# Attention and two dense layers on one core: a third early operand buffer, output copies on one engine, and new durations in the plan

## The chip, the cores and the metric

The kernel runs on one core of one Trainium2 chip. The metric is the device time of one execution in microseconds (us); lower is better. A core has a matmul engine (TensorE, PE in the rows, with its weight loads as PEld), VectorE (DVE), ScalarE (ACT), GpSimd (POOL) and SyncE (SP), which here issues the transfers between memory and on-chip buffers.

## What is computed

Attention over blocks of 64 tokens (a token sees its own block and all earlier ones), then a gated layer, then a second layer with the activation called ELU, all in 32-bit floats:

```python
scores = scale * q @ k.T            # 4 batches, 8 heads, 576 tokens, 64 channels
attn = softmax(where(block_i >= block_j, scores, -1e9)) @ v
x = attn as (2304 tokens, 512)
g = x @ w_gate; val = x @ w_val     # 512 -> 1536
y = (g * sigmoid(g) * val) @ w_out  # 1536 -> 512, the first output product
h = y @ w_in                        # 512 -> 2048
out = where(h > 0, h, exp(min(h, 0)) - 1) @ w_out2   # 2048 -> 512
```

## The kernel before

**Split products.** Every operand of a large product is cut into a high half, rounded to the matmul engine's own 32-bit form, and a low half, the rest. A product is three matmuls: high x high, high x low, low x high (`mm3`, L163 to L166). Making the halves is the work of the other engines: ACT writes the high half, DVE or POOL subtracts it for the low one.

**Stages.** (1) Attention for chunks of 256 tokens, and beside it the gate and value products, called gv; their result is stored in the scratch tensor a_scr. (2) The first output product, called p2: five chunks (four of 512 tokens, one of 256), each of 12 units, one for each block of 128 of the 1536 channels. A unit loads its operand (`ar`, L663), ACT writes `ah` (L666), DVE writes `al` (L669), and the PE issues 4 x 3 matmuls into four accumulators y. The ring of ah and al has three slots, so unit n can be split once unit n - 3 has been multiplied. Two of the slots lie in space that comes free when attention ends (`to_w1`), the third in space that comes free when gv ends (`to_p2`). After 12 units `p2_drain` copies the four accumulators to `ys` (L708), two on ACT and two on DVE, and SP stores them to y_scr. (3) The second layer, called p3, for three groups of 768 tokens and 8 pairs of channel blocks each. It uses a seven-product scheme for 2 x 2 blocks: `p3_y` combines and splits y (L749, L757, L758), `p3_weights` does the same for the input weights (L793, L801, L804, stored in w_scr), `p3_h` multiplies, adds up on DVE (L854, seven sums to a pair), applies ELU (L845 to L848) and splits the result into `gh` (ACT, L849) and `gl` (DVE, L851). `p3_o` multiplies by the output weights of the pair before.

**Weights** arrive as 64-bit floats. `conv_unit` turns one block into 32-bit: a load of 512 KB (`raw`), one step on ACT (L142), three on DVE (L150, L152, L154), and for a plain weight the high half on ACT (L157) and the low one on POOL (L161). There are 68 such units: 24 for gate and value, 12 for the first output weights (`wo`, tiles woh and wol), 32 for the last two weights. A unit of the last output weight is converted into place during p2 if its pair is below NE, else during p3.

**What sets the order.** `Plan` is a list scheduler that runs when the program is built. Each task has an engine, a duration in ns written in the code, a priority and its dependences; `Plan.order` walks through time and always starts the ready task of the best priority. From this comes one fixed order of instructions on each engine. On the chip each engine takes its instructions in that order and waits at each for what it needs. The durations in the code decide only the order; the chip's own decide the time.

Of the kernel before, what the change touches and what calls it, by code (L numbers as in the profile page):

```python
# [8 lines left out]
F32 = mybir.dt.float32  # L9
# [25 lines left out]
GF, NACT, NFP, XLP = 4, 20, 8, False  # L35
NFILL, PFILL, WARM = 40, 1e9, 7000.0
CLEAD2, CLEAD3 = 5.0, 100.0
HT, NG, HP, PAIR3, NP, NW, NE = 384, 3, K2 // 2, 15.4, 9, 8, 5
LAT, SELF, DMA_IN, DMA_OUT = 300.0, 100.0, 1300.0, 900.0


# [69 lines left out]
def attention_moe_moe_kernel(ctx: ExitStack, tc: tile.TileContext,  # L111
# [116 lines left out]
    def conv_unit(i, prio, after=(), whole=False):  # L228
        r, c, w = ("raw", i, 0), ("c", i, 0), ("w", i, 0)
        add("SP", 450, lambda: cv_dma(i), prio, writes=[r], data=1456)  # L230
        add("ACT", 520, lambda: cv_a(i), prio, [r], [c])
        for p, ns in enumerate((335, 602, 602)):
            add("DVE", ns, lambda p=p: cv_b(i, p), prio, [r, c], [c])
        if whole:
            return
        add("ACT", 520, lambda: cv_hi(i), prio, [c], [w], after)
        add("POOL", 1330, lambda: cv_lo(i), prio, [c, w], [w])


    qz = [t0.tile([128, H, 128], F32, name=f"qz{u}") for u in range(2)]  # L240
# [416 lines left out]
    def p2_prep(i, T, f):  # L657
        u, v = nxt("ar"), nxt("ah")
        late = [("p2", 0, 0)]

        def load():
            for j in range(T // CH):
                sp.dma_start(out=ar_b[u % 5][:, CH * j:CH * j + CH], in_=a_scr[2 * i + j][f])  # L663

        def hi():
            act.activation(ah_b[v % 3][:, 0:T], ar_b[u % 5][:, 0:T], ACTF.Copy, scale=0.5)  # L666

        def lo():
            dve.scalar_tensor_tensor(al_b[v % 3][:, 0:T], ar_b[u % 5][:, 0:T], 0.5, ah_b[v % 3][:, 0:T].bitcast(F32), ALU.mult, ALU.subtract)  # L669

        ark, ahk = ("ar", u, 0), ("ah", v, 0)
        add("SP", 450 * (T // CH), load, PMP, [("a", (2 * i + j) * K1 + f // 2 * 2, 0) for j in range(T // CH)], [ark],
            [("w1", 0, 0)] if u < 3 else late, data=T * 1.42)
        add("ACT", .833 * T + 93, hi, PMP, [ark], [ahk], [] if v < 2 else late)
        add("DVE", 1.04 * T + 68, lo, PMP, [ark, ahk], [("ah", v, 1)])
        return v

    yacc = {}
# [23 lines left out]
    def p2_drain(i, T):  # L702
        for m in range(KD):
            u = nxt("ys")
            yk, k = ("y", i * KD + m, 0), ("ys", u, 0)

            def cp(eng, m=m, u=u):
                eng(ys_b[u % 4][:, 0:T], yacc[i, m][:, 0:T])  # L708

            def spill(g, c, t, n, m=m, u=u):  # L710
                sp.dma_start(out=y_scr[g][m, :, c:c + n], in_=ys_b[u % 4][:, t:t + n])

            plan.group = "p2"
            add(*(("ACT", .833 * T + 90, lambda cp=cp: cp(act.copy)) if m % 2 else ("DVE", 1.04 * T + 68, lambda cp=cp: cp(dve.tensor_copy))), PMP,
                [yk], [k], [("p2", 0, 0)])
            for x in p2_parts(i, T):
                add("SP", 450, lambda x=x, spill=spill: spill(*x), PMP, [k], [("yscr", x[0], (m, i))], data=x[3] * 1.42)
            plan.group = None
# [64 lines left out]
    def p3_weights(p, prio):  # L783

        i = unit["i", 2 * p]
        for u in range(2):
            conv_unit(i + u, prio, whole=True)
        part = lambda r, c: cv_state[i + r][1][:, 256 * c:256 * c + 256]
        ck = lambda r, c: ("c", i + r, c)
        whole = [("c", i, 0), ("c", i + 1, 0)]  # L790

        def comb(d, x, y, op):
            add("DVE", 400, lambda: dve.tensor_tensor(part(*d), part(*x), part(*y), op), prio, [ck(*x), ck(*y)] + whole, [ck(*d)])  # L793

        def split(o, x):
            n = nxt("wm")
            hk, lk = ("wm", n, 0), ("wm", n, 1)

            def hi():
                wm[n] = hand["wp"].tile([128, 2, 256], F32R, tag="wm", name="wm", bufs=3)  # L800
                act.copy(wm[n][:, 0], part(*x))  # L801

            add("ACT", 400, hi, prio, [ck(*x)] + whole, [hk], [("p2", 0, 0)])
            add("POOL", 850, lambda: pool.tensor_tensor(wm[n][:, 1], part(*x), wm[n][:, 0].bitcast(F32), ALU.subtract), prio, [ck(*x), hk] + whole, [lk])  # L804
            add("SP", 450, lambda: sp.dma_start(out=w_scr[p][o], in_=wm[n].bitcast(F32).rearrange("p h f -> p (h f)")), prio - 1,
                [hk, lk], [("wscr", p, o)], data=728)
# [12 lines left out]
        split(6, a11)
# [11 lines left out]
    def p3_h(i, p, ns, due):  # L831
# [7 lines left out]
        def elu(src, sk, name):  # L839
# [4 lines left out]
            g = lambda k: gp[v % NP][k]  # L844
            add("ACT", 500, lambda: act.activation(t(), src(), ACTF.Tanh, scale=0.5), PMP, [sk], [tk], first)  # L845
            add("ACT", 500, lambda: act.activation(e(), src(), ACTF.Exp), PMP, [sk], [ek])
            add("DVE", 540, lambda: dve.scalar_tensor_tensor(t(), e(), 1.0, t(), ALU.add, ALU.mult), PMP, [tk, ek], [tk])  # L847
            add("DVE", 540, lambda: dve.scalar_tensor_tensor(t(), t(), 0.0, src(), ALU.min, ALU.max), PMP, [tk, sk], [tk])  # L848
            add("ACT", 480, lambda: act.copy(g(0), t()), PMP, [tk], [hk], first)  # L849
            eng, en = dve, "DVE"  # L850
            add(en, 1100 if eng is pool else 540, lambda: eng.tensor_tensor(g(1), t(), g(0).bitcast(F32), ALU.subtract), PMP, [tk, hk], [lk])  # L851

        def plus(b, x, d):
            add("DVE", 520, lambda: dve.tensor_tensor(hc(d), hb[b][:, 0:HT], hc(x), ALU.add), PMP, [hbk(b), hck(x)], [hck(d)])  # L854

        for o, j in enumerate(OSEQ):
            b = (7 * q + o) % 2 if q or o < 2 else o
# [73 lines left out]
    def to_w1():  # L931
        attn.release()
        at_ps.release()
        hand["st2"] = sb("st2", 1, "right")
        p2_bufs(hand["st2"], (0, 1, 2), (0, 1))
        hand["w1"] = sb("w1", 1, "right")
        hand["y_ps"] = ps("y_ps", 1, "right")
        for g in range(K1):
            WOH[g] = hand["w1"].tile([128, DM], F32R, name=f"woh{g}")
            WOL[g] = hand["w1"].tile([128, DM], F32R, name=f"wol{g}")  # L940
            cv_units[2 * K1 + g] = (wo[g], WOH[g], WOL[g])

    def to_p2():
        hand["wgvB"].release()
# [3 lines left out]
        gv_ps.release()  # L948
        hand["st3"] = sb("st3", 1)
        p = hand["st3"]  # L950
        p2_bufs(p, (3, 4), (2,))
        ys_b.extend(p.tile([128, 512], F32, name=f"ys{k}") for k in range(4))
        p = hand["wp"] = sb("wp", 1)
        for f in range(2 * NE):
# [154 lines left out]
```

## Time and profile before

| | us |
|---|---|
| median of 3 runs | 1061.53 (1060.5 to 1070.12) |
| the profiled execution | 1062.92 |
| its span, first to last instruction | 1061.2 |
| PE busy | 1030.2 |
| DVE busy | 837.1 |
| ACT busy | 599.2 |
| POOL busy | 292.7 |

Busy time is an average over stages with different limits: what a change in one stage is worth is read in that stage's stretch. Matmuls overlap and their ends are modelled, so the steps from start to start tell more than PE's busy time. The granted clock is full (1.00) in every stretch quoted below.

### The profile page before, as it was taken

How to read it: one execution, taken by the hardware profiler on the slowest of the kernel's cores; microseconds unless marked ns; L12 is line 12 of the kernel's file. 1: busy time of each engine (PE TensorE's matmuls, PEld its weight loads, DVE VectorE, ACT ScalarE, POOL GpSimd, SP SyncE). 2: the span in 40 equal slices, each digit the busy share in tenths (PEclk: the TensorE clock that was granted, in tenths of full speed). 3: DMA queues.
4: the chain of work that ended last, by engine and by line, in shares of the span. 5: the costliest groups of instructions: out<-in, count | busy, mean ns of one | idle time of the engine just before them, and what ended most of it. 6: DMA issues, size and time to landing. Idle time of an engine off the chain costs nothing. (4 is left out here: it accounts for less than half of the span.)

```text
span 1061.2 us, 19577 instructions
## 1 busy us (share of the span) xinstructions
PE 1030.2 (97%) x6520; PEld 934.1 (88%) x6520; DVE 837.1 (79%) x1977; ACT 599.2 (56%) x1521; POOL 292.7 (28%) x288
## 2 busy tenths in 40 slices
PE   8999899999999999999999999999999999999998
PEld 7678899999999999999877778888988989898997
DVE  6689998888888888878777787798678665876664
ACT  4688787777776776654454544545344433543342
POOL 1268544443443344303234333331000000000000
PEclk8899999999999999999999999999999999999999
DMA  7487556432442244014799888874446434454331
GB/s 176 135 232 208 159 165 185 119 90 86 125 126 85 87 125 119 32 54 147 248 328 313 299 274 304 300 234 129 120 133 215 128 111 119 129 169 114 115 109 61
DMA packets 119366, 170.00 MB, mean 160 GB/s; under 512 B 15840, under 2 KB 75744, under 8 KB 119264
## 3 DMA queue, kind: packets, MB, share of 16 engines
q1 hardware_dynamic: 119264, 168.74, 52.5%
q8 instruction: 52, 0.85, 0.3%
q14 instruction: 50, 0.41, 0.1%
HBM read 130.42 MB, written 38.27 MB: 159 GB/s over the span
## 5 line engine op out<-in xcount | busy, mean ns | idle before, releaser
L164 PE MATMUL gv<-xh,wh 128*128 128x256 f32 x864 | 257.1, 298 | 1.1 <-DVE as L645 0.8
L165 PE MATMUL gv<-xl,wh 128*128 128x256 f32 x864 | 242.4, 281 | 0.1
L166 PE MATMUL gv<-xh,wl 128*128 128x256 f32 x864 | 242.1, 280 | 0.0
L164 PEld LDWEIGHTS gv<-xh,wh 128*128 128x128 f32 x864 | 164.2, 190 | 7.4 <-issue 4.3
L165 PEld LDWEIGHTS gv<-xl,wh 128*128 128x128 f32 x864 | 164.3, 190 | 0.5 <-DVE xl L604 0.3
L166 PEld LDWEIGHTS gv<-xh,wl 128*128 128x128 f32 x864 | 164.0, 190 | 0.0
L854 DVE TENSOR_TENSOR ys<-h,ys 128x384 f32<-128x384 f32 x162 | 88.0, 554 | 83.4 <-PE h L166 78.4
L845 ACT ACTIVATE ar<-ys 128x384 f32<-128x384 f32 x96 | 50.5, 526 | 134.0 <-DVE ys L854 111.9
L164 PE MATMUL h<-yo,ws 128*128 128x384 f32 x326 | 110.0, 337 | 1.9 <-DVE ys L854 1.7
L165 PE MATMUL h<-yo,ws 128*128 128x384 f32 x326 | 110.0, 337 | 0.0
L166 PE MATMUL h<-yo,ws 128*128 128x384 f32 x326 | 109.6, 336 | 0.0
L165 PE MATMUL y<-al,woh 128*128 128x512 f32 (+1 forms) x240 | 89.5, 373 | 5.8 <-DVE al L669 5.7
L409 POOL TENSOR_TENSOR ks<-rk,ks 64x576 fp32r<-64x576 f32 (+1 forms) x56 | 70.7, 1262 | 88.1 <-ACT ks L406 46.9
L164 PE MATMUL y<-ah,woh 128*128 128x512 f32 (+1 forms) x240 | 88.9, 370 | 2.3 <-ACT ys L708 1.0
L166 PE MATMUL y<-ah,wol 128*128 128x512 f32 (+1 forms) x240 | 88.4, 368 | 0.0
L804 POOL TENSOR_TENSOR wm<-c,wm 128x256 fp32r<-128x256 f32 x56 | 55.5, 1002 | 96.9 <-ACT wm L801 87.1
L894 PE MATMUL o<-oh,gl 128*128 128x512 f32 x198 | 78.8, 398 | 1.8 <-DVE gl L851 1.6
L893 PE MATMUL o<-ol,gh 128*128 128x512 f32 x198 | 78.1, 395 | 0.0
L892 PE MATMUL o<-oh,gh 128*128 128x512 f32 x198 | 77.1, 389 | 0.5 <-ACT gh L849 0.5
L542 DVE TENSOR_TENSOR tl<-tr,th 128x256 fp32r<-128x256 f32 x176 | 69.1, 415 | 6.9 <-ACT th L538 6.1
L538 ACT CAST th<-tr 128x256 fp32r<-128x256 f32 x176 | 61.3, 376 | 22.5 <-PE tr L534 20.6
L422 POOL TENSOR_TENSOR vs<-rv,vs 128x320 fp32r<-128x320 f32 (+1 forms) x56 | 48.0, 857 | 94.1 <-ACT vs L418 80.9
(150 smaller groups left out, 2654.1 us busy)
## 6 DMA issues: line engine op xcount, KB each, us to landing
ws<-w_scr SPq DMA_DIRECT2D x168, 256.0 KB, 2.7
w_scr<-wm SPq DMA_DIRECT2D x56, 256.0 KB, 3.8
a_scr<-as SPq DMA_DIRECT2D x54, 256.0 KB, 2.4
ar<-a_scr SPq DMA_DIRECT2D x108, 128.0 KB, 3.7
rk<-in_kt_dram SPq DMA_DIRECT2D x32, 288.0 KB, 4.4
raw<-in_w2i_dram SPq DMA_DIRECT2D x16, 512.0 KB, 4.5
raw<-in_w2o_dram SPq DMA_DIRECT2D x16, 512.0 KB, 5.0
rq<-in_qt_dram SPq DMA_DIRECT2D x60, 128.0 KB, 3.9
```

Source lines behind the costliest of these rows:

```text
L164: pe.matmul(dst, wh, xh, start=start, stop=False)
L165: pe.matmul(dst, wh, xl, start=False, stop=False)
L166: pe.matmul(dst, wl, xh, start=False, stop=stop)
L409: pool.tensor_tensor(st["ks"][64:128, 0:ext], raws[i][0][64:128, j, 0:ext], st["ks"][64:128, 0:ext].bitcast(F32), ALU.subtract)
L538: act.copy(st["th", c], st["tr", c][:, 0:QW])
L542: dve.tensor_tensor(st["tl", c], st["tr", c][:, 0:QW], st["th", c].bitcast(F32), ALU.subtract)
L804: add("POOL", 850, lambda: pool.tensor_tensor(wm[n][:, 1], part(*x), wm[n][:, 0].bitcast(F32), ALU.subtract), prio, [ck(*x), hk] + whole, ...
L845: add("ACT", 500, lambda: act.activation(t(), src(), ACTF.Tanh, scale=0.5), PMP, [sk], [tk], first)
L854: add("DVE", 520, lambda: dve.tensor_tensor(hc(d), hb[b][:, 0:HT], hc(x), ALU.add), PMP, [hbk(b), hck(x)], [hck(d)])
L892: pe.matmul(d, h, OH[f], start=(p == 0 and u < 2), stop=False)
L893: pe.matmul(d, h, OL[f], start=False, stop=False)
L894: pe.matmul(d, l, OH[f], start=False, stop=(p == HP - 1 and u > 1))
```

## The change

Five things are changed. The third slot of ah and al is allocated with the other two when attention ends; in return the last of the twelve wo tiles is allocated, and its halves are written, only when gv has ended (`wo_alloc`). All copies of `p2_drain` go to ACT. The plan's durations are raised for what runs from the wo units on: the conversion's three DVE steps, the low halves on POOL, `al`, the weight recombination, and DVE's steps of p3. NE goes from 5 to 3, so four more units of the last output weight (two pairs) are converted in p3 and not in p2. NP, the number of gate slots in p3, goes from 9 to 8.

```diff
-HT, NG, HP, PAIR3, NP, NW, NE = 384, 3, K2 // 2, 15.4, 9, 8, 5
+HT, NG, HP, PAIR3, NP, NW, NE = 384, 3, K2 // 2, 15.4, 8, 8, 3
...
-        for p, ns in enumerate((335, 602, 602)):
+        for p, ns in enumerate((335, 602, 602) if i < 2 * K1 else (500, 700, 750)):
             add("DVE", ns, lambda p=p: cv_b(i, p), prio, [r, c], [c])
...
-        add("POOL", 1330, lambda: cv_lo(i), prio, [c, w], [w])
+        add("POOL", 1330 if i < 2 * K1 else 1500, lambda: cv_lo(i), prio, [c, w], [w])
...
-        add("ACT", .833 * T + 93, hi, PMP, [ark], [ahk], [] if v < 2 else late)
-        add("DVE", 1.04 * T + 68, lo, PMP, [ark, ahk], [("ah", v, 1)])
+        add("ACT", .833 * T + 93, hi, PMP, [ark], [ahk], [] if v < 3 else late)
+        add("DVE", 1.3 * T + 68, lo, PMP, [ark, ahk], [("ah", v, 1)])
...
-            add(*(("ACT", .833 * T + 90, lambda cp=cp: cp(act.copy)) if m % 2 else ("DVE", 1.04 * T + 68, lambda cp=cp: cp(dve.tensor_copy))), PMP,
-                [yk], [k], [("p2", 0, 0)])
+            add("ACT", .833 * T + 90, lambda cp=cp: cp(act.copy), PMP, [yk], [k], [("p2", 0, 0)])
...
-            add("DVE", 400, lambda: dve.tensor_tensor(part(*d), part(*x), part(*y), op), prio, [ck(*x), ck(*y)] + whole, [ck(*d)])
+            add("DVE", 500, lambda: dve.tensor_tensor(part(*d), part(*x), part(*y), op), prio, [ck(*x), ck(*y)] + whole, [ck(*d)])
```

In the same way the plan's 850 becomes 1000 for the weight split on POOL (L804), 540 becomes 575 for the three DVE steps of ELU and its split, and 520 becomes 560 for the sums (L854). The buffers:

```diff
     def to_w1():
...
-        p2_bufs(hand["st2"], (0, 1, 2), (0, 1))
+        p2_bufs(hand["st2"], (0, 1, 2), (0, 1, 2))
...
-        for g in range(K1):
-            WOH[g] = hand["w1"].tile([128, DM], F32R, name=f"woh{g}")
-            WOL[g] = hand["w1"].tile([128, DM], F32R, name=f"wol{g}")
-            cv_units[2 * K1 + g] = (wo[g], WOH[g], WOL[g])
+        for g in range(K1 - 1):
+            wo_alloc(hand["w1"], g)
+
+    def wo_alloc(p, g):
+        WOH[g] = p.tile([128, DM], F32R, name=f"woh{g}")
+        WOL[g] = p.tile([128, DM], F32R, name=f"wol{g}")
+        cv_units[2 * K1 + g] = (wo[g], WOH[g], WOL[g])
 
     def to_p2():
...
-        p2_bufs(p, (3, 4), (2,))
+        p2_bufs(p, (3, 4), ())
+        wo_alloc(p, K1 - 1)
...
-        conv_unit(2 * K1 + g, due2[0, g] - CLEAD2, after=[("w1", 0, 0)])
+        conv_unit(2 * K1 + g, due2[0, g] - CLEAD2, after=[("w1" if g < K1 - 1 else "p2", 0, 0)])
```

Since the durations steer the plan, the order of instructions changes on every engine, from the attention stage on. Three places follow; the lines of the changed kernel are one lower here (L792 is L793 before).

DVE in p2, at the 41st to 43rd al (L669, unit by unit), before; c is a weight block in conversion, raw its loaded words:

```order
L669 SCALAR_TENSOR_TENSOR al_8169<-ar_8163,ah_8167 128x512
L150 TENSOR_SCALAR c<-c 128x512
L152 SCALAR_TENSOR_TENSOR c<-raw,c 128x512
L154 SCALAR_TENSOR_TENSOR c<-raw,c 128x512
L669 SCALAR_TENSOR_TENSOR al_8722<-ar_8164,ah_8721 128x512
L150 TENSOR_SCALAR c<-c 128x512
L152 SCALAR_TENSOR_TENSOR c<-raw,c 128x512
L154 SCALAR_TENSOR_TENSOR c<-raw,c 128x512
L669 SCALAR_TENSOR_TENSOR al_8168<-ar_8165,ah_8166 128x512
```

The same place in the changed kernel:

```order
L669 SCALAR_TENSOR_TENSOR al_8170<-ar_8163,ah_8167 128x512
L792 TENSOR_TENSOR c<-c 128x256
L152 SCALAR_TENSOR_TENSOR c<-raw,c 128x512
L150 TENSOR_SCALAR c<-c 128x512
L154 SCALAR_TENSOR_TENSOR c<-raw,c 128x512
L669 SCALAR_TENSOR_TENSOR al_8171<-ar_8164,ah_8168 128x512
L152 SCALAR_TENSOR_TENSOR c<-raw,c 128x512
L154 SCALAR_TENSOR_TENSOR c<-raw,c 128x512
L669 SCALAR_TENSOR_TENSOR al_8169<-ar_8165,ah_8166 128x512
```

Between the 41st and 42nd al and again between the 42nd and 43rd stood three conversion steps; now a recombination and three steps stand in the first gap and two steps in the second.

ACT at the end of the first chunk of p2, before; oh is a converted weight, wm a recombined one:

```order
L666 ACTIVATE ah_8167<-ar_8719 128x512
L801 CAST wm<-c 128x256
L142 ACTIVATE c<-raw 128x512
L708 COPY ys_8724<-y 128x512
L708 COPY ys_8726<-y 128x512
L666 ACTIVATE ah_8721<-ar_8720 128x512
L142 ACTIVATE c<-raw 128x512
```

and in the changed kernel:

```order
L666 ACTIVATE ah_8167<-ar_8725 128x512
L800 CAST wm<-c 128x256
L708 COPY ys_8729<-y 128x512
L708 COPY ys_8730<-y 128x512
L708 COPY ys_8731<-y 128x512
L708 COPY ys_8732<-y 128x512
L666 ACTIVATE ah_8168<-ar_8726 128x512
```

Two copies to ys behind a conversion step (L142) became four, behind a cast of wm; the next ah stands behind the four.

DVE in p3, from the 21st sum (L854) on, before:

```order
L854 TENSOR_TENSOR ys_8724<-h_8763,ys_8724 128x384
L154 SCALAR_TENSOR_TENSOR c<-raw,c 128x512
L847 SCALAR_TENSOR_TENSOR ar_8163<-ar_8165,ar_8163 128x384
L851 TENSOR_TENSOR gl_10218<-ar_8164,gh_10217 128x384
L848 SCALAR_TENSOR_TENSOR ar_8163<-ar_8163,ys_8725 128x384
L150 TENSOR_SCALAR c<-c 128x512
L152 SCALAR_TENSOR_TENSOR c<-raw,c 128x512
L154 SCALAR_TENSOR_TENSOR c<-raw,c 128x512
L851 TENSOR_TENSOR gl_10220<-ar_8163,gh_10219 128x384
L847 SCALAR_TENSOR_TENSOR ar_8164<-ar_8719,ar_8164 128x384
L749 TENSOR_TENSOR yq_10689<-yq_8751,yq_8750 128x768
L848 SCALAR_TENSOR_TENSOR ar_8164<-ar_8164,ys_8724 128x384
```

and in the changed kernel (L853 is the sum, L846, L847 and L850 the steps of ELU and of its split):

```order
L853 TENSOR_TENSOR ys_8730<-h_8761,ys_8730 128x384
L154 SCALAR_TENSOR_TENSOR c<-raw,c 128x512
L846 SCALAR_TENSOR_TENSOR ar_8163<-ar_8165,ar_8163 128x384
L850 TENSOR_TENSOR gl_10183<-ar_8164,gh_10182 128x384
L847 SCALAR_TENSOR_TENSOR ar_8163<-ar_8163,ys_8731 128x384
L150 TENSOR_SCALAR c<-c 128x512
L152 SCALAR_TENSOR_TENSOR c<-raw,c 128x512
L846 SCALAR_TENSOR_TENSOR ar_8164<-ar_8725,ar_8164 128x384
L850 TENSOR_TENSOR gl_10185<-ar_8163,gh_10184 128x384
L847 SCALAR_TENSOR_TENSOR ar_8164<-ar_8164,ys_8730 128x384
L154 SCALAR_TENSOR_TENSOR c<-raw,c 128x512
L853 TENSOR_TENSOR ys_8730<-h_8761,ys_8729 128x384
```

The recombination of y (L749 on yq) and the next conversion's first step (L150) have left this place; they stand further on.

## Rows read from the trace of the kernel before

**Rows 1.** The page's busy time, share of the span and instructions of each engine

```profile
PE 1030.2 (97%) x6520; PEld 934.1 (88%) x6520; DVE 837.1 (79%) x1977; ACT 599.2 (56%) x1521; POOL 292.7 (28%) x288
```

**Rows 2.** Windows: stretch and its length, each engine's busy time, clock, transfers

```profile
core 0: us, PE busy (x) PEld busy (x) DVE busy (x) ACT busy (x) POOL busy (x), PEclk, DMA share, GB/s
140.00:480.00 340.00, 337.11 (x2825) 332.68 (x2824) 290.99 (x932) 238.49 (x716) 134.53 (x144) 1.00 0.37 105
515.50:653.50 138.00, 130.29 (x561) 104.03 (x560) 107.35 (x152) 66.67 (x129) 50.92 (x47) 1.00 0.89 302
673.30:730.00 56.70, 52.65 (x253) 44.33 (x253) 53.61 (x91) 30.36 (x67) 19.77 (x17) 1.00 0.71 235
752.50:768.00 15.50, 15.50 (x79) 13.96 (x78) 9.60 (x20) 5.96 (x13) 0.00 (x0) 1.00 0.38 114
```

**Rows 3.** Waits of PE, 515.5 to 653.5 us: total us, times, longest us

```profile
PE y L165 <- DVE al L669: 5.7, 7, 1.4
PE y L164 <- ACT ys L708: 1.0, 1, 1.0
PE y L164 <- DVE ys L708: 1.0, 2, 0.6
```

**Rows 4.** Timeline of PE: start us, duration us, instruction [idle before <- who ended it]

```profile
587.65 0.39 PE L165 MATMUL y<-al,woh 128*128 128x512 f32 x1
...
600.80 0.39 PE L166 MATMUL y<-ah,wol 128*128 128x512 f32 x1
...
636.97 0.39 PE L164 MATMUL y<-ah,woh 128*128 128x512 f32 x1
638.40 0.50 PE L165 MATMUL y<-al,woh 128*128 128x512 f32 x1 [1.04 <-DVE al L669]
```

**Rows 5.** Timeline of DVE at that stop

```profile
634.73 1.07 DVE L150 TENSOR_SCALAR c<-c 128x512 int32<-128x512 int32 x1 [0.65 <-ACT c L142]
635.83 0.69 DVE L152 SCALAR_TENSOR_TENSOR c<-raw,c 128x512 int32<-128x512 int32 x1
636.55 1.19 DVE L154 SCALAR_TENSOR_TENSOR c<-raw,c 128x512 int32<-128x512 int32 x1
637.67 0.68 DVE L669 SCALAR_TENSOR_TENSOR al<-ar,ah 128x512 fp32r<-128x512 f32 x1
```

**Rows 6.** Timeline of ACT at three places of p2

```profile
548.37 0.66 ACT L142 ACTIVATE c<-raw 128x512 f32<-128x512 f32 x1 [3.60 <-DMA raw<-in_w2o_dram]
548.93 1.06 ACT L708 COPY ys<-y 128x512 f32<-128x512 f32 x2
...
598.40 0.84 ACT L757 CAST yo<-yq 128x768 fp32r<-128x768 f32 x1 [4.31 <-DMA yq<-y_scr]
...
634.60 0.62 ACT L666 ACTIVATE ah<-ar 128x512 fp32r<-128x512 f32 x1
```

**Rows 7.** Groups by line, whole span: count | busy us, mean ns | idle before

```profile
L152 DVE SCALAR_TENSOR_TENSOR c<-raw,c 128x512 int32<-128x512 int32 x68 | 56.5, 831 | 1.0
L154 DVE SCALAR_TENSOR_TENSOR c<-raw,c 128x512 int32<-128x512 int32 x68 | 56.1, 826 | 0.6
L150 DVE TENSOR_SCALAR c<-c 128x512 int32<-128x512 int32 x68 | 40.6, 599 | 14.5 <-ACT c L142 14.3
L749 DVE TENSOR_TENSOR yq<-yq,yq 128x768 f32<-128x768 f32 x12 | 13.9, 1158 | 2.8 <-DMA yq<-y_scr 2.8
L708 DVE COPY ys<-y 128x512 f32<-128x512 f32 (+1 forms) x10 | 6.3, 630 | 3.0 <-PE y L166 3.0
L708 ACT COPY ys<-y 128x512 f32<-128x512 f32 (+1 forms) x10 | 5.1, 543 | 1.7 <-PE y L166 1.6
```

**Rows 8.** Waits of PE, 673.3 to 730 us

```profile
PE o L894 <- DVE gl L851: 1.6, 2, 1.2
```

**Rows 9.** Timeline of POOL and of DVE around 719 us

```profile
718.61 1.83 POOL L161 TENSOR_TENSOR ol<-c,oh 128x512 fp32r<-128x512 f32 x1 [4.55 <-ACT oh L157]
...
719.31 1.67 DVE L152 SCALAR_TENSOR_TENSOR c<-raw,c 128x512 int32<-128x512 int32 x1
```

More of the change, by code (lines that the diff above doesn't have):

```diff
@@ L803, in split @@
             add("ACT", 400, hi, prio, [ck(*x)] + whole, [hk], [("p2", 0, 0)])
-            add("POOL", 850, lambda: pool.tensor_tensor(wm[n][:, 1], part(*x), wm[n][:, 0].bitcast(F32), ALU.subtract), prio, [ck(*x), hk] + whole, [lk])
+            add("POOL", 1000, lambda: pool.tensor_tensor(wm[n][:, 1], part(*x), wm[n][:, 0].bitcast(F32), ALU.subtract), prio, [ck(*x), hk] + whole, [lk])
             add("SP", 450, lambda: sp.dma_start(out=w_scr[p][o], in_=wm[n].bitcast(F32).rearrange("p h f -> p (h f)")), prio - 1,
@@ L846, in elu @@
             add("ACT", 500, lambda: act.activation(e(), src(), ACTF.Exp), PMP, [sk], [ek])
-            add("DVE", 540, lambda: dve.scalar_tensor_tensor(t(), e(), 1.0, t(), ALU.add, ALU.mult), PMP, [tk, ek], [tk])
-            add("DVE", 540, lambda: dve.scalar_tensor_tensor(t(), t(), 0.0, src(), ALU.min, ALU.max), PMP, [tk, sk], [tk])
+            add("DVE", 575, lambda: dve.scalar_tensor_tensor(t(), e(), 1.0, t(), ALU.add, ALU.mult), PMP, [tk, ek], [tk])
+            add("DVE", 575, lambda: dve.scalar_tensor_tensor(t(), t(), 0.0, src(), ALU.min, ALU.max), PMP, [tk, sk], [tk])
             add("ACT", 480, lambda: act.copy(g(0), t()), PMP, [tk], [hk], first)
             eng, en = dve, "DVE"
-            add(en, 1100 if eng is pool else 540, lambda: eng.tensor_tensor(g(1), t(), g(0).bitcast(F32), ALU.subtract), PMP, [tk, hk], [lk])
+            add(en, 1100 if eng is pool else 575, lambda: eng.tensor_tensor(g(1), t(), g(0).bitcast(F32), ALU.subtract), PMP, [tk, hk], [lk])
         def plus(b, x, d):
-            add("DVE", 520, lambda: dve.tensor_tensor(hc(d), hb[b][:, 0:HT], hc(x), ALU.add), PMP, [hbk(b), hck(x)], [hck(d)])
+            add("DVE", 560, lambda: dve.tensor_tensor(hc(d), hb[b][:, 0:HT], hc(x), ALU.add), PMP, [hbk(b), hck(x)], [hck(d)])
         for o, j in enumerate(OSEQ):
```

## The prediction

> **What bounds the kernel now.** The first view is the page's table of engines: the matmul engine (PE) is busy 97% of the span, so no other engine can be the bound over long [rows 1]. That figure hides short stops, because the end of a matmul is modelled; so I read the views in this order: windows by stage, who the PE waited for, and the timeline at a stop.
>
> In the windows the stretch 140 to 480 us (attention and first stage) has the PE busy 337.11 of 340.00 us: at most 2.9 us are to be had there. Two stretches stand out, 515.5 to 653.5 us, most of the first output product (called p2 in the code), and 673.3 to 730 us, the first pairs of the last stage (p3) [rows 2].
>
> In p2 the stretch holds 561 matmuls of 512 columns and nothing else. From the row at 587.65 us to the row at 600.80 us 58 steps pass with no stop, 13.15 us, 0.2267 us each [rows 4]. So 561 take 127.2 us, and the stretch lasts 138.0: the PE loses 10.8 us. The list of waits says to whom: 5.7 us in 7 stops for the low half of the split operand (al, VectorE, L669), 2.0 us in 3 stops for the copy that empties an accumulator (ys, L708) [rows 3]. These 7.7 us are the idle time; the rest of the 10.8 is the slow restart after a stop. Shared out in proportion, al costs 8.0 us and ys 2.8 us.
>
> In p3 the reference is the window 752.5 to 768, where the PE issues 79 matmuls in 15.5 us, about one pair, with no stop. At that rate the 253 matmuls of 673.3 to 730 take 49.6 us, but it lasts 56.7: 7.1 us lost. VectorE (DVE) is busy 53.61 of these 56.7 us, against 9.60 of 15.5 in the quiet window [rows 2]; the PE waits there for gl, a DVE result [rows 8]. So the DVE bounds that stretch: weight conversions and recombinations stand in it beside the pairs' own work.
>
> **What a stop in p2 looks like.** At 638.40 us the PE had been idle 1.04 us for al [rows 4]. Its high half ah was written on ScalarE (ACT) from 634.60 for 0.62 us, so by 635.2 [rows 6]. The DVE began al at 637.67, because three conversion steps stood ahead of it, at 634.73, 635.83 and 636.55, lasting 1.07, 0.69 and 1.19 us: 2.95 us [rows 5]. The plan had counted 335 + 602 + 602 ns, 1.54 us. A second kind of stop is no matter of planned DVE times: ACT stands idle 4.31 us before the yo copy at 598.40, waiting for a transfer, and the next ah is queued behind it [rows 6].
>
> **The change part by part.**
>
> *Measured durations.* A conversion's three DVE steps are planned as 500, 700 and 750 ns, together 1.95 us; the means are 599, 831 and 826, together 2.26 us [rows 7]. The plan was short by 0.72 us per conversion and is now short by 0.31. The order shows what follows: at the place of the stop just read, three conversion steps between two al become two. The second kind of stop stays: in the new order ACT's yo copy stands one unit later, and its transfer is again issued shortly behind the eight spill transfers of the chunk before. So of the 8.0 us I take less than half as saved, 3.5 us. Bounds: nothing saved, if the stops only change places, and 8.0 if all go.
>
> *The ten DVE copies.* They go to ACT: 10 x 0.630 us leave the DVE, 10 x 0.543 us come to ACT [rows 7], which is busy 66.67 of 138.0 us in p2 [rows 2]. As work this costs nothing; what counts is the queue. Before, a DVE copy could stand behind conversion steps that wait; now four copies stand in a row on ACT behind one 256-column cast. ACT has its own long wait: 3.60 us for a transfer ahead of the conversion step at 548.37, with the two copies at 548.93 behind it [rows 6], and that was the longest ys stop, 1.0 us on the PE [rows 3]. In the new order no such step stands directly ahead of the first four copies, but at the second chunk one does. I take 2.0 of the 2.8 us as saved. Bounds: 2.8 saved, or 3.6 lost, if such a wait now holds all four copies of a chunk at once.
>
> *Third buffer early, last wo tile late.* The ring was and stays three deep; its third slot is only there sooner, during the last gv matmuls. In the order this brings one more group of three y matmuls (3 x 0.227 = 0.68 us) ahead of the end of gv. The fourth split still needs the end of gv and a load after it, and the PE then has that 0.68 us less in hand. Moved work is not gained work: zero, bounds 0.7 either way. The wo tile now converted after gv is used by the twelfth unit, 11 x 12 x 0.227 = 30 us on; that cover hides its conversion.
>
> *Four conversions from p2 to p3* (NE from 5 to 3). In p2 they free 4 x 2.26 = 9.0 us of DVE time; the DVE was busy 107.35 of 138.0 us there [rows 2], so this counts only through the stops above. In p3 I counted the new order along the DVE's sum rows (L854 before, seven to a pair). Up to the 24th, about where the 7.1 us were lost, it holds as many conversion steps as before and two wide recombinations (L749, mean 1.16 us [rows 7]) fewer: 2.3 us less in a stretch that the DVE bounds. With the planned times of the pair's own DVE steps raised too, I take 2.5 us saved. The moved work stands at sums 25 to 40: 9.0 us and the two recombinations, 11.3 us together. Those are 2.3 pairs, and a quiet pair leaves the DVE 15.5 - 9.60 = 5.9 us [rows 2], 13.6 us in all. It fits, so it costs nothing; that slack is its only cover. Bounds for p3: 7.1 saved to 12.4 lost (below).
>
> *Eight gate slots for nine* (NP). Eight slots are two pairs of four; a pair's gates are read while the next pair computes, so a slot is free again before the pair after that writes it. Zero.
>
> *Attention and first stage.* The plan's new numbers reorder these too. The PE is 99% busy there; zero, bounds 2.9 either way.
>
> **Sum.** 3.5 + 2.0 + 2.5 = 8.0 us. The profiled execution took 1062.92 us, which would become 1054.9; it lies 1.4 us above the median of the three runs, 1061.53. Against the median: **1053.5 us**.
>
> **The rivals.**
> - *Nearly all stops go.* With true durations the plan puts every al early enough: 7.0 of the 8.0, 2.5 of the 2.8 and 4.6 of the 7.1, together 14.1 us: 1047.4. For it: the stop at 638.40 is wholly a planning error, and the DVE's load in p2 falls by 9.0 + 6.3 us. Against it: the planned 1.95 us is still under 2.26, and the yo wait is untouched.
> - *Nothing but a new order.* The stops in p2 come from transfers: ACT's waits of 3.60 and 4.31 us are for transfers [rows 6], in a stretch where the transfer engines are 89% busy [rows 2]. The changed numbers describe DVE, ACT and POOL, not transfers; the stops change places: 1061.5. Against it: 5.7 of 7.7 us are put down to DVE.
> - *Slower: the moved conversions hit p3.* Their price if nothing hides them is 9.0 us, and each brings a POOL subtraction: at 718.61 POOL ran one for 1.83 us, and the DVE step begun at 719.31 took 1.67 us, 0.84 above its mean [rows 9, 7]. Four such holds are 3.4 us: 12.4 us in all, and with the p2 gain of 5.5 kept, 1061.5 - 5.5 + 12.4 = 1068.4. It decides once the work at sums 25 to 40 exceeds the 13.6 us free: 11.3 + 3.4 = 14.7 is 1.1 over, so a small overflow is near, the full price only with a DVE that is already behind at the 24th sum.
>
> The Trainium skill speaks for this last rival: "SBUF — State Buffer", section "Who interferes with whom", says that a DVE instruction with two SBUF inputs and a GpSimd instruction reading SBUF exclude each other, and whichever issues second waits for the whole of the first. The row agrees: the DVE step ended at 720.98, 0.54 us after POOL's 720.44. By that rule a hold can last a whole 1.83 us, four of them 7.3 us, an estimate from that row, and the rival would end at 1072.3.
>
> **How the numbers follow.** Forecast 0.50 (its own range 1049 to 1058), nearly all stops gone 0.24, nothing but a new order 0.16, slower 0.10. The range reaches to the other cases: 1047.4 less the 2.9 us of the first stages gives 1044.5 below; above, half way from no gain to the slower case, 1065. A measurement of this kernel tells about 1% from no change: 1050.9 and 1072.1. Under 1050.9 lie most of the second case and the low edge of the forecast, 0.20 + 0.11 = 0.31; above 1072.1 the far half of the slower case, 0.05; between them 0.64.
>
> **What would show it.** In p2 the PE's wait for al falls from 5.7 us to about 3 and that for ys under 0.6, with all 20 copies on ACT. In p3 the last conversion comes near the 37th sum, some 80 us into the stage instead of some 53, the DVE stays about 90% busy over five pairs, and the loss to the quiet rate falls from 7.1 to about 4.5 us. The forecast is wrong if the waits for al stand as before behind other steps (then the plan's durations were not the cause), if one ACT wait holds four copies, or if the PE stops at sums 25 to 40.

## The result, and the profile after

| | before | after |
|---|---|---|
| first comparison, median of 4 runs each, us | 1061.01 | 1047.01 (1042.26 to 1054.75) |
| ratio, 95% interval | | 0.9876 [0.9837, 0.9914] |
| repeat (a1_after below), medians, us | 1060.01 | 1044.58 |
| ratio, 95% interval | | 0.9855 [0.983, 0.988] |

The change makes the kernel 1.2 to 1.5% faster, 14.0 us in the first comparison and 15.4 us in the repeat; 8.0 us were forecast. The time lies inside the predicted range (1044.5 to 1065) and beside the rival "nearly all stops go" (1047.4), outside the forecast's own 1049 to 1058. The profiled execution of the first comparison was the slowest of its four (1054.75 us, span 1053.0), so the profile of the repeat (span 1042.1) stands beside it.

The page's first part, after, answers to [rows 1]: the DVE lost 9.8 us of work, ACT gained 4.2, PE lost 4.3 us of modelled busy time.

```profile
PE 1025.9 (97%) x6520; PEld 935.2 (89%) x6520; DVE 827.3 (79%) x1967; ACT 603.4 (57%) x1531; POOL 297.2 (28%) x288
```

Windows of the kernel after, its stages 2 to 5 us earlier; they answer to [rows 2]. Columns as there.

```profile
140.00:480.00 340.00, 336.70 (x2829) 333.22 (x2828) 289.59 (x932) 237.69 (x717) 133.19 (x144) 1.00 0.38 105
513.70:647.00 133.30, 128.65 (x558) 103.86 (x557) 95.50 (x137) 66.59 (x132) 51.30 (x46) 1.00 0.89 301
668.50:725.20 56.70, 54.08 (x269) 47.46 (x268) 51.01 (x92) 32.45 (x71) 21.21 (x16) 1.00 0.79 258
668.50:747.50 79.00, 76.38 (x380) 67.65 (x379) 72.54 (x131) 45.48 (x98) 25.48 (x19) 1.00 0.73 235
```

The same stretch of p2 in the repeat's profile:

```profile
510.10:637.50 127.40, 126.63 (x559) 104.34 (x558) 97.41 (x139) 67.38 (x132) 47.41 (x45) 1.00 0.93 316
```

At the quiet step of 0.2267 us [rows 4], 558 matmuls take 126.5 us: the PE loses 6.8 us in p2 in the one execution and 0.7 us in the other, where it lost 10.8 before. In the first 56.7 us of p3, 269 matmuls at 15.5 / 79 us each take 52.8: 3.9 us lost, 7.1 before. All that follows is read in this measure, a stretch's length less its matmuls at the quiet rate. It tells stages apart; of single executions it can tell only differences above the 6 us just seen between two of the same kernel, so the verdicts below go by medians, and what a single profile is read for is a wait at one place that comes back in other profiles.

Waits of PE in 500 to 670 us of the kernel after, with total us, times, longest us, and the copies' group; they answer to [rows 3] and [rows 7]:

```profile
PE y L165 <- DVE al L669: 3.7, 8, 0.7
PE y L164 <- ACT ah L666: 2.7, 3, 1.6
...
L708 ACT COPY ys<-y 128x512 f32<-128x512 f32 (+1 forms) x20 | 10.3, 545 | 2.6 <-PE y L166 2.2
```

No wait for ys is left, and all 20 copies stand on ACT.

### The profile page after: what moved, and what is told of

Its sections match the earlier page's. It is cut to its first block, busy times and chain, and to the rows that moved or that the text cites. A ratio compares the mean times of both kernels' runs of the same rounds, so it can differ in the third digit from the quotient of the medians.

```text
span 1053.0 us, 19578 instructions
## 1 busy us (share of the span) xinstructions
PE 1025.9 (97%) x6520; PEld 935.2 (89%) x6520; DVE 827.3 (79%) x1967; ACT 603.4 (57%) x1531; POOL 297.2 (28%) x288
## 5 line engine op out<-in xcount | busy, mean ns | idle before, releaser
L853 DVE TENSOR_TENSOR ys<-h,ys 128x384 f32<-128x384 f32 x162 | 88.5, 554 | 75.4 <-PE h L166 67.2
L803 POOL TENSOR_TENSOR wm<-c,wm 128x256 fp32r<-128x256 f32 x56 | 61.0, 1101 | 103.3 <-ACT wm L800 87.3
L893 PE MATMUL o<-oh,gl 128*128 128x512 f32 x180 | 71.5, 397 | 0.5 <-DVE gl L850 0.5
L892 PE MATMUL o<-ol,gh 128*128 128x512 f32 x180 | 71.1, 395 | 0.0
L891 PE MATMUL o<-oh,gh 128*128 128x512 f32 x180 | 70.2, 390 | 0.8 <-ACT gh L848 0.8
```

The costliest lines, as they stand in the source:

```text
L803: add("POOL", 1000, lambda: pool.tensor_tensor(wm[n][:, 1], part(*x), wm[n][:, 0].bitcast(F32), ALU.subtract), prio, [ck(*x), hk] + whole, ...
L853: add("DVE", 560, lambda: dve.tensor_tensor(hc(d), hb[b][:, 0:HT], hc(x), ALU.add), PMP, [hbk(b), hck(x)], [hck(d)])
L891: pe.matmul(d, h, OH[f], start=(p == 0 and u < 2), stop=False)
L892: pe.matmul(d, h, OL[f], start=False, stop=False)
L893: pe.matmul(d, l, OH[f], start=False, stop=(p == HP - 1 and u > 1))
```

## The experiments

Three parts of the change can be made alone: D, the new durations; C, the copies on ACT; B, the buffers with NE 3 and NP 8. The medians are of 4 (b2_dvedrain), 6 (a1_after, c3_after_shuffle, c4_dur_ylate) or 11 to 12 runs, in three batches, each beside its own runs of the kernel before. Of longer edits the diffs show the telling lines.

| kernel | parts | median, us | before, us | ratio | 95% interval |
|---|---|---|---|---|---|
| a2_dur | D | 1053.78 | 1060.01 | 0.9939 | [0.992, 0.9958] |
| a3_drain | C | 1058.28 | 1060.01 | 0.9979 | [0.9958, 1.0] |
| a4_buf | B | 1060.62 | 1060.01 | 1.0001 | [0.9978, 1.0024] |
| b1_olddur | B, C | 1061.69 | 1061.04 | 1.0024 | [0.9999, 1.0049] |
| b4_durdrain | D, C | 1055.51 | 1061.04 | 0.9957 | [0.9933, 0.998] |
| b2_dvedrain | D, B | 1044.44 | 1061.04 | 0.9854 | [0.9834, 0.9873] |
| a1_after | D, B, C | 1044.58 | 1060.01 | 0.9855 | [0.983, 0.988] |
| b5_shuffle | none, other order | 1056.69 | 1061.04 | 0.9955 | [0.993, 0.998] |
| c3_after_shuffle | D, B, C, same order (see below) | 1047.19 | 1060.6 | 0.9864 | [0.9826, 0.9902] |
| c1_ne5 | D, B, C, but NE 5 | 1052.48 | 1060.6 | 0.9921 | [0.9896, 0.9946] |
| c2_dur_ne3 | D, NE 3 | 1054.95 | 1060.6 | 0.9944 | [0.992, 0.9968] |
| c4_dur_ylate | D, yq planned later | 1046.99 | 1060.6 | 0.9861 | [0.9828, 0.9895] |

**The change again, and each part alone.** a1_after is the changed kernel. The others make one part of its diff on the kernel before.

> The changed kernel once more, five rounds beside the kernel before, to fix the size of the whole gain. The forecast's sum says 8.0 us less than before (about 1053); the first runs gave about 13 us. If the surplus was luck of single executions it comes out near 8; if it is real, near 13, and the trace should show where the further 5 us lie outside the stretches that the forecast counted.

a2_dur, the duration lines, of which these are two:

```diff
-        for p, ns in enumerate((335, 602, 602)):
+        for p, ns in enumerate((335, 602, 602) if i < 2 * K1 else (500, 700, 750)):
...
-        add("DVE", 1.04 * T + 68, lo, PMP, [ark, ahk], [("ah", v, 1)])
+        add("DVE", 1.3 * T + 68, lo, PMP, [ark, ahk], [("ah", v, 1)])
```

> The kernel before with the plan's new durations alone (buffers, copies, NE and NP as before). Theory of the forecast: the waits for the low half in the first output product and the DVE-bound start of the last stage come from conversions planned too short, so this alone gives most of the gain: 3.5 + about 2.5 = 6 us. Rival (mere reordering): the durations have no merit of their own, the stops change places, 0 us with 3 either way. Rival (third slot): the gain hangs on the early third slot, so 0 here.

a3_drain, the copies:

```diff
-            add(*(("ACT", .833 * T + 90, lambda cp=cp: cp(act.copy)) if m % 2 else ("DVE", 1.04 * T + 68, lambda cp=cp: cp(dve.tensor_copy))), PMP,
+            add("ACT", .833 * T + 90, lambda cp=cp: cp(act.copy), PMP,
```

> The kernel before with all twenty output copies on ACT and nothing else. Forecast: 2.0 us less, the PE's stops for ys (2.0 us idle before) nearly gone. Rival (mere reordering): any size within 3 us, with the ys stops replaced by stops for ah or al.

a4_buf, the buffers:

```diff
-HT, NG, HP, PAIR3, NP, NW, NE = 384, 3, K2 // 2, 15.4, 9, 8, 5
+HT, NG, HP, PAIR3, NP, NW, NE = 384, 3, K2 // 2, 15.4, 8, 8, 3
...
-        p2_bufs(hand["st2"], (0, 1, 2), (0, 1))
+        p2_bufs(hand["st2"], (0, 1, 2), (0, 1, 2))
```

> The kernel before with the buffers alone: third slot early, last wo tile late, four conversions moved to the last stage, eight gate slots; old durations, old copies. Forecast: the third slot gives nothing; the moved conversions relieve the first output product but, with the old durations, stand where the DVE bounds the last stage: between 2 us saved and 4 us lost. Rival (third slot carries the gain): 5 us or more saved, most of it before and at the end of the gate and value products.

Alone the parts are worth -6.2, -1.7 and +0.6 us, 7.3 us in all, close to the forecast's 8.0. Together they are worth 15.4. So the surplus over the forecast lies in an interaction, unless it is luck of the order, which comes after the next three.

**Which parts interact.** Each of the next three leaves one part of the changed kernel out: b1_olddur the durations, b2_dvedrain the copies, b4_durdrain the buffers.

```diff
-        for p, ns in enumerate((335, 602, 602) if i < 2 * K1 else (500, 700, 750)):
+        for p, ns in enumerate((335, 602, 602)):
```

> The changed kernel with the old durations back: buffers and copies only. The single parts alone gave 6.2 us (durations), 1.7 (copies) and nothing (buffers), 8 together; the whole gives 15. If the missing 7 us come from copies and buffers helping each other, this run saves 7 us or more. If they need the durations (the four conversions find room in the last stage only where the plan knows how long they take), it saves about 2.

```diff
-            add("ACT", .833 * T + 90, lambda cp=cp: cp(act.copy), PMP,
+            add(*(("ACT", .833 * T + 90, lambda cp=cp: cp(act.copy)) if m % 2 else ("DVE", 1.04 * T + 68, lambda cp=cp: cp(dve.tensor_copy))), PMP,
```

> The changed kernel with half of the output copies back on DVE: durations and buffers. If the 7 us beyond the sum of the parts come from durations and buffers together, this saves about 13 us; if the copies are needed for it, about 6. Mere reordering would put it anywhere between 4 and 14 with no stretch of the trace to show for it.

```diff
-        p2_bufs(hand["st2"], (0, 1, 2), (0, 1, 2))
+        p2_bufs(hand["st2"], (0, 1, 2), (0, 1))
...
-        p2_bufs(p, (3, 4), ())
+        p2_bufs(p, (3, 4), (2,))
```

> The kernel before with new durations and all copies on ACT, old buffers (third slot late, NE 5, NP 9). If durations and copies make the surplus, this saves about 15 us; if the buffers (the four conversions moved out of the first output product) are needed for it, about 8, the sum of the two parts.

Durations and buffers carry it: D with B is 0.9854, and the copies add nothing to it. Without D the rest is worth nothing (1.0024), without B no more than D alone (0.9957).

**How much is luck of the order.** b5_shuffle changes the planned conversion steps of all weights from the first output weight on by a few ns, in the kernel before:

```diff
-        for p, ns in enumerate((335, 602, 602)):
+        for p, ns in enumerate((335, 602, 602) if i < 2 * K1 else (340, 600, 600)):
```

> Control for mere reordering: the kernel before with the conversion's planned 335, 602, 602 ns changed to 340, 600, 600 from the first output weight on, the same sum within 1 ns, so a new order with no better knowledge. Forecast: within 2 us of the kernel before. Rival (mere reordering): a gain or loss of 4 us or more, which would make gains of that size worth nothing as evidence.

c3_after_shuffle was meant to do the same in the changed kernel. Its edit is not the same: it changes the steps of the gate and value weights.

```diff
-        for p, ns in enumerate((335, 602, 602) if i < 2 * K1 else (500, 700, 750)):
+        for p, ns in enumerate((340, 600, 600) if i < 2 * K1 else (500, 700, 750)):
```

> A control: the changed kernel with the planned durations of the three steps of a first-layer weight's conversion set from 335, 602, 602 to 340, 600, 600 ns, which means nothing but another order of the same work. The same edit in the kernel before was worth 4.4 us. Theory (the surplus of the new durations and the buffers together is theirs, and not the luck of one order): 1042 to 1049, ratio 0.983 to 0.989. Rival (the changed kernel's order is a lucky draw, about 5 us better than what these edits give on the average): 1049 to 1053, ratio 0.989 to 0.993.

Another order of the same work is worth 4.4 us in the kernel before, so 4 us between two kernels of this plan prove no mechanism. For the changed kernel there is no such control: in the trace of c3_after_shuffle the instructions of every engine (6520 matmuls, 1967 of the DVE, 1531 of ACT) stand in the very order of the changed kernel. It is the changed kernel measured a third time (1047.19). That the 9 us from D alone to D with B are more than luck of the draw is therefore not shown by a control, only made likely by further orders: three with D and the late slot have ratios of 0.9939 to 0.9957 (a2_dur, c2_dur_ne3, b4_durdrain), two with D and all of B 0.9854 and 0.9855 (b2_dvedrain, a1_after).

**Where the interaction sits.** In D alone the stops of p2 are all still there. The stretch of p2 in a2_dur:

```profile
508.60:646.40 137.80, 130.29 (x557) 104.76 (x557) 105.83 (x151) 65.81 (x128) 54.57 (x46) 0.99 0.91 300
```

557 matmuls take 126.3 us, so 11.5 us are lost, against 10.8 before. ScalarE's timeline there (start us, duration us, instruction, idle before and what ended it) shows the costliest place:

```profile
582.95 0.63 ACT L666 ACTIVATE ah<-ar 128x512 fp32r<-128x512 f32 x1 [2.08 <-PE y L166]
583.49 0.39 ACT L801 CAST wm<-c 128x256 fp32r<-128x256 f32 x1
591.22 0.83 ACT L757 CAST yo<-yq 128x768 fp32r<-128x768 f32 x1 [7.34 <-DMA yq<-y_scr]
591.95 1.15 ACT L666 ACTIVATE ah<-ar 128x512 fp32r<-128x512 f32 x2
```

ACT stands 7.34 us at a copy of yq, whose transfer has not landed, and the next two operands are queued behind it: 9.0 us between two ah, while a unit is used up in 12 x 0.227 = 2.7 us. The PE loses 4.1 us here: from the matmul at 590.69 us to the one at 597.05 ten steps take 6.36 us and not 2.27 (the rows of the stop stand in the last section). In D with B the first copies of yq come with operands before and between them (b2_dvedrain):

```profile
590.61 0.84 ACT L757 CAST yo<-yq 128x768 fp32r<-128x768 f32 x1 [1.17 <-DMA yq<-y_scr]
591.35 0.62 ACT L666 ACTIVATE ah<-ar 128x512 fp32r<-128x512 f32 x1
...
592.18 0.63 ACT L666 ACTIVATE ah<-ar 128x512 fp32r<-128x512 f32 x1
595.62 2.31 ACT L757 CAST yo<-yq 128x768 fp32r<-128x768 f32 x3 [2.81 <-DMA yq<-y_scr]
```

Where the first of these copies stands in ACT's order, counted in ah from p2's first one, goes with the wait in all 14 profiles:

| behind ah number | kernels | wait for yq there, us |
|---|---|---|
| 30 | a2_dur, b4_durdrain, c2_dur_ne3, b1_olddur | 6.05 to 7.34 |
| 31 | before, a3_drain, a4_buf, b5_shuffle, c4_dur_ylate | 3.73 to 4.65 |
| 32 | after, a1_after, c3_after_shuffle, b2_dvedrain, c1_ne5 | 0.49 to 1.17 |

That is the interaction, read from the order itself: D alone puts the copy one unit earlier than before, B alone leaves it, D with the early slot puts it one unit later. A place later takes some 2 to 3.5 us off the wait; a unit lasts 2.7.

Three experiments part the causes: the slot without the four moved conversions (c1_ne5), the moved conversions without the slot (c2_dur_ne3), and neither, but ACT's copies of yq later in the order (c4_dur_ylate), by planning the transfer longer:

```diff
-                [("yq", r, 0)], [("p2", 0, 0)], data=1100)
+                [("yq", r, 0)], [("p2", 0, 0)], data=4000)
```

The plan adds 2.2 us of its own to such a time (`DMA_IN`, `DMA_OUT`), so it counted 3.3 us and now counts 6.2; in 520 to 680 us of the kernel before these transfers took 6.2 us (median of 8).

> The kernel before with the new durations, and the transfer of the finished sums (yq) planned at 4000 ns in place of 1100, which is near the 2.8 to 7.3 us that the longest ones are waited for; it puts ScalarE's copies of yq one or two operand steps later, so that the operands of the first output product no longer stand behind such a wait. No buffer is changed. Theory of the slot (what the first output product lacks is the third slot): 1053.8 as with the new durations alone, ratio 0.992 to 0.996, stops in the first output product 10 us or more. Rival (it is the wait for the transfer ahead of the operands in ScalarE's queue, which the changed kernel shortens from 9.0 to 3.7 us in all): 1046 to 1049, ratio 0.986 to 0.990, stops down from 12 to about 5 us, with ScalarE's waits for yq near 3 us.

The changed kernel with

```diff
-HT, NG, HP, PAIR3, NP, NW, NE = 384, 3, K2 // 2, 15.4, 8, 8, 3
+HT, NG, HP, PAIR3, NP, NW, NE = 384, 3, K2 // 2, 15.4, 8, 8, 5
```

> The changed kernel with NE back at 5: third operand slot, late seventh output weight, new durations, all copies on ScalarE stay, but the four conversions are made in the first output product again. Theory of the slot (the early third slot and the late weight, which need the new durations to bring anything, make the surplus): the time stays at the changed kernel's 1044.6 to 1047, less the 2.5 us that the four conversions cost in the last stage's start, which may come back, so 1042 to 1048, ratio 0.982 to 0.988; the stops of the first output product after its start stay at 3 to 5 us. Rival (the four conversions and their eight raw transfers crowd the first output product, and taking them out is what the new durations needed): back to the 1053.8 of the new durations alone, ratio 0.992 to 0.996, with about 12 us of stops in the first output product.

(The late weight, called the seventh there, is the twelfth.) The kernel before with D and

```diff
-HT, NG, HP, PAIR3, NP, NW, NE = 384, 3, K2 // 2, 15.4, 9, 8, 5
+HT, NG, HP, PAIR3, NP, NW, NE = 384, 3, K2 // 2, 15.4, 9, 8, 3
```

> The kernel before with the new durations and NE 3 (four conversions moved to the last stage), NP 9, no early third slot, no late weight, copies on both engines. The mirror of the run with NE at 5. Theory of the slot: 1053.8 as with the new durations alone, ratio 0.992 to 0.996, and the 2.5 to 2.8 us of stops where the first output product begins are still there. Rival (the conversions): 1044 to 1047, ratio 0.984 to 0.988, stops in the first output product down from 12 to 3 to 5 us. If each half gives some, both runs come out near 1049, ratio near 0.989.

c4_dur_ylate gains as much as the whole change, with no buffer added: 1046.99 us. The theory that the gain needs the slot falls with it; the rival, the wait ahead of the operands in ACT's queue, had 1046 to 1049. ACT's timeline in c4_dur_ylate at the same place:

```profile
583.96 0.64 ACT L666 ACTIVATE ah<-ar 128x512 fp32r<-128x512 f32 x1 [0.34 <-PE y L166]
585.39 0.41 ACT L801 CAST wm<-c 128x256 fp32r<-128x256 f32 x1 [0.80 <-DVE c L154]
586.73 0.63 ACT L666 ACTIVATE ah<-ar 128x512 fp32r<-128x512 f32 x1 [0.93 <-PE y L166]
591.53 0.83 ACT L757 CAST yo<-yq 128x768 fp32r<-128x768 f32 x1 [4.17 <-DMA yq<-y_scr]
592.27 0.63 ACT L666 ACTIVATE ah<-ar 128x512 fp32r<-128x512 f32 x1
```

The transfer is there at nearly the same time, 591.5 us for 591.2, but ACT comes to it one operand later, at 587.4 for 583.9. It waits 4.17 us and not 7.34, 5.5 us pass between two ah, and the PE does not stop here. In all of p2 the PE's waits for al and ah fall from 4.8 + 2.6 us in a2_dur to 2.2 + 1.1 us.

Yet c4_dur_ylate is no clean test of the wait alone. Its stretch of p2, then the PE in it:

```profile
508.80:641.90 133.10, 129.80 (x571) 106.17 (x570) 98.80 (x141) 63.42 (x121) 47.29 (x41) 1.00 0.89 299
599.85 0.39 PE L166 MATMUL y<-ah,wol 128*128 128x512 f32 x1
600.08 0.33 PE L164 MATMUL h<-yo,ws 128*128 128x384 f32 x1
600.25 0.34 PE L165 MATMUL h<-yo,ws 128*128 128x384 f32 x1
```

The new order also pulls the first 12 matmuls of p3 (h) into p2, from 600.08 to 602.19 us: 2.1 us of work for the PE, while the DVE makes the next al from 600.15 us on. With these 2.1 us and 559 matmuls of p2 at the quiet step, 4.3 us are lost, for 11.5 in a2_dur. Of the 7.2 us between them 4.1 are the stop behind the wait for yq. Another stop of a2_dur, 2.43 us for al at 611.94, is gone too; whether the later copy or the 12 matmuls took it away was not tried, and this order has no reordering control either.

In p2 it is the slot and not the moved conversions. The stretch of p2 in c1_ne5, then in c2_dur_ne3:

```profile
510.90:641.10 130.20, 128.07 (x558) 103.99 (x558) 103.06 (x139) 69.11 (x134) 51.11 (x46) 1.00 0.92 310
```

```profile
513.70:652.60 138.90, 130.36 (x558) 103.44 (x557) 98.10 (x147) 63.66 (x126) 50.50 (x46) 1.00 0.90 299
598.53 0.83 ACT L757 CAST yo<-yq 128x768 fp32r<-128x768 f32 x1 [6.48 <-DMA yq<-y_scr]
```

With the slot 3.7 us are lost; ACT waits for yq in two pieces, 1.03 and 2.52 us. Without it 12.4 us are lost, and the long wait for yq (6.48 us) is back, though c2 moved the same four conversions away. These two differ in NP and in the copies as well, but the pairs that differ in the slot, the late weight and NP alone say the same: b4_durdrain loses 10.4 us in p2 with a first wait for yq of 6.05 us, c1_ne5 3.7 with 1.03; c2_dur_ne3 loses 12.4 with 6.48, b2_dvedrain 3.2 with 1.17. So in the changed kernel it is the early slot, by the order that it lets the plan make, that shortens this wait. It also counts where p2 begins: in 505 to 525 us the PE stands idle for ah and al 1.8 to 2.4 us in the four kernels with D and the late slot (c4_dur_ylate is one), 0.5 to 0.8 in the five with D and the early one.

Yet c1_ne5 as a whole misses the 1042 to 1048 that the slot's theory gave it: it loses 8.4 us in the first 56.7 us of p3 (246 matmuls), more than half of it at one stop. First the DVE's timeline there, then the PE's:

```profile
678.06 0.56 DVE L853 TENSOR_TENSOR ys<-o,ys 128x384 f32<-128x384 f32 x1 [0.63 <-PE o L166]
682.01 0.96 DVE L748 TENSOR_TENSOR yq<-yq,yq 128x768 f32<-128x768 f32 x1 [3.39 <-DMA yq<-y_scr]
...
684.49 0.55 DVE L853 TENSOR_TENSOR ys<-h,ys 128x384 f32<-128x384 f32 x1
```

```profile
685.10 0.69 PE L164 MATMUL h<-yo,ws 128*128 128x384 f32 x1 [4.31 <-DVE ys L853]
```

It is the same pattern on another engine: the DVE stands 3.39 us at a step that wants yq, the sum that frees an accumulator is queued behind, and the PE stops 4.31 us. NE 5 by itself does not bring this stop: a2_dur and b4_durdrain have it too and lose 2.9 and 2.0 us in that stretch. It belongs to this one order; why the order came out so is open. In time the slot, the late weight and NP are worth about 10 us with NE 3 (c2_dur_ne3 to b2_dvedrain) and about 3 with NE 5 (b4_durdrain to c1_ne5).

**What is left in p2.** The two profiles of the changed kernel differ by 6 us there, and ACT's timeline of the first shows where (the PE stopped 1.64 us for ah at 627.58):

```profile
620.67 0.41 ACT L800 CAST wm<-c 128x256 fp32r<-128x256 f32 x1 [4.24 <-DMA w_scr<-wm]
...
626.35 0.66 ACT L142 ACTIVATE c<-raw 128x512 f32<-128x512 f32 x1 [4.20 <-DMA raw<-in_w2i_dram]
```

These are waits of the same kind for two other transfers, and c3_after_shuffle, whose profiled run was its slowest (1051.95 us) and lost 8.4 us in p2, has them too (4.23 and 4.81 us). In the repeat's profile ACT waits nowhere in 600 to 640 us over 3.0 us for a transfer. The order is the same in all three; so whether they come is decided by when the transfers land in that execution. Longer planned times for these two transfers were not tried.

No kernel tried beats the changed one beyond the measurement: b2_dvedrain equals it. The changed kernel with yq planned later as well was not run.

## Why the prediction was right, and where its steps failed

**What came as forecast.** The wait for al fell from 5.7 us to 3.7 us, in the stretch 515.5 to 653.5 us to 2.4 (forecast about 3); ys is gone. But the wait for ah rose from 0.2 to 2.7 us, so that in this execution the PE's idle time in p2 fell only from 7.9 to 6.4 us; in the repeat's profile 1.6 us for al are all that is left. In p3 the loss fell to 3.9 us (forecast about 4.5), with the DVE 72.54 of 79.0 us busy, 92%. The last conversion's last step began here, 81.6 us after p2's last product at 668.3 (forecast some 80):

```profile
749.87 0.68 DVE L154 SCALAR_TENSOR_TENSOR c<-raw,c 128x512 int32<-128x512 int32 x1
```

The slower rival did not come: no wait of PE is on record from 718 to 765 us, where the moved conversions stand. Holds by POOL did occur there:

```profile
746.31 1.69 POOL L161 TENSOR_TENSOR ol<-c,oh 128x512 fp32r<-128x512 f32 x1 [8.52 <-ACT oh L157]
...
746.76 1.79 DVE L152 SCALAR_TENSOR_TENSOR c<-raw,c 128x512 int32<-128x512 int32 x1
```

The DVE step took 1.79 us against a mean of 0.90, and ended 0.55 us after POOL's end at 748.00, as at 719 us before [rows 9]; POOL's spans are rough. That is how the Trainium skill has it in "SBUF — State Buffer", section "Who interferes with whom": a DVE instruction with two SBUF inputs and a GpSimd instruction that reads SBUF exclude each other for a whole instruction. The slack of 13.6 us took the hold in.

**The number was the rival's.** The time came beside "nearly all stops go" (1047.4), but not by its mechanism: with the new durations alone p2 keeps its stops. That the range reached down to it covers a gain whose cause the prediction did not have; in that it was luck.

**Measured durations, 3.5 us.** With the 2.5 us of p3 that their planned times share in, 6.0; alone they gave 6.2, but in another place. In p2 D alone saves nothing: 11.5 us lost against 10.8. Its gain is where the forecast set zero or named another cause. By the start-to-start steps beyond the quiet ones, D takes off 1.2 us in 140 to 480 us, 1.8 from 480 to the end of gv, and 3.8 in the first 100 us of p3: 6.8 us. The same three in the changed kernel are 0.5, 1.8 and 2.8 (1.3, 1.8 and 2.6 in the repeat).

**The second kind of stop.** The prediction saw ACT's wait of 4.31 us for yq [rows 6], said that it stays, and so held the durations to less than half of 8.0 us. It had even counted that the copy stands one unit later in the new order, and gave that no worth, because the transfer is issued late again. This is the step that failed: a unit more ahead of the copy goes with a wait 2 to 3.5 us shorter (the table above). The one wait of 4.31 us became two, of 0.85 and 2.81 us (0.54 and 1.69 in the repeat), with operands between them, and the PE does not stop there. With D alone the copy stands a unit earlier, the wait grows to 7.34 us, and nothing of the 8.0 is gained. That was also the argument held against the rival "nearly all stops go": the yo wait was not untouched, the early slot beside D moved it.

**Third slot early, 0 us.** Right alone (B: 1.0001), wrong beside D, by about 10 us with NE 3. "Moved work is not gained work" is true of work; but a slot that comes free earlier changes what is ready, and so the order of everything behind it. In D with B the copies of yq meet their transfer late enough, and the start of p2, where the prediction allowed 0.7 us either way, is 1.0 to 1.9 us shorter of idle time than with D and the late slot.

**Copies, 2.0 us.** Alone 1.7 us, with an interval that just reaches no change; in the whole nothing, since D with B leaves a single ys wait of 0.6 us, on the DVE.

**Four conversions, 2.5 us.** The gain in p3 came, but not from them: a2_dur, with NE at 5, has 274 matmuls in the first 56.7 us of p3, so it loses 2.9 us; a4_buf, with the conversions moved and the old durations, loses 5.1 us there, but over the first 100 us of p3 as much as before, and gains nothing in time. The new planned times carried it; which of them, the conversions' or those of the pair's own DVE steps, which the prediction named in half a sentence, was not tried.

## What to carry to other kernels

Where a planned order feeds in-order queues, look in the trace for an instruction that waits several microseconds for a transfer on an engine that also feeds the bound one, and plan that transfer as long as it takes; here that one number came with a gain of about 7 us over the new durations alone, not much less than the early slot and the moved conversions gave. In p2 correct durations paid nothing while that wait stood ahead of the operands, so parts of such a change must not be added up. And measure what a mere reordering does before a few microseconds are given a cause, and look in the trace whether the control has changed the order at all.

## What the runs showed of the hardware

**A stop can cost more than itself.** In a2_dur the PE stood still up to 592.63 us, and its next matmuls came at steps of 0.43 us and not 0.227:

```profile
592.63 0.51 PE L164 MATMUL y<-ah,woh 128*128 128x512 f32 x1 [1.55 <-ACT ah L666]
593.69 0.79 PE L165 MATMUL y<-al,woh 128*128 128x512 f32 x1 [0.56 <-DVE al L669]
594.28 0.63 PE L166 MATMUL y<-ah,wol 128*128 128x512 f32 x1
594.71 0.63 PE L164 MATMUL y<-ah,woh 128*128 128x512 f32 x1
...
611.94 0.50 PE L165 MATMUL y<-al,woh 128*128 128x512 f32 x1 [2.43 <-DVE al L669]
```

Windows of PE with the granted clock (after the count):

```profile
593.60:596.60 3.00, 2.91 (x7) 0.50 1.05 409
...
612.00:616.00 4.00, 4.00 (x18) 1.00 0.71 227
```

After the stops of 1.55 and 0.56 us the clock was at its lower level, 1.2 GHz, and the steps stayed long until 596.8 (in 597 to 601 us it was 1.00 again); after the longer one of 2.43 us at 611.94 it stayed at 2.4 GHz. After c1_ne5's stop of 4.31 us it was 0.60 on the mean of 685 to 689 us. What decides it, these runs don't show.

**The start differs between executions of one kernel.** Windows of 20 to 40 us, of the changed kernel's first profile and of its repeat:

```profile
20.00:40.00 20.00, 19.79 (x89) 14.65 (x89) 13.60 (x45) 13.08 (x38) 5.33 (x4) 0.74 0.36 111
```

```profile
20.00:40.00 20.00, 19.16 (x107) 13.19 (x107) 17.42 (x53) 16.52 (x49) 7.42 (x5) 1.00 0.54 166
```

The clock was 0.74 in the one and full in the other, and 89 against 107 matmuls were done; the kernel before had 0.61 there. Times of one kernel spread by up to 15 us (b1_olddur, 1057.72 to 1072.79), and mostly go with the mean clock: of b4_durdrain's twelve runs the fastest had 0.996 and 1050.42 us, the slowest 0.986 and 1061.51. So spans of single profiles say little by themselves. In p2, too, three executions of the very same order lost 0.7, 6.8 and 8.4 us.
